# Splitting an MLP's matrix products into 64x64 pieces on the quarters of the TensorE array, in a kernel that runs a recurrence beside it

**Chip, cores, metric.** One core of one Trainium2 chip. The metric is device time in microseconds (us) of the whole kernel; lower is better. A profile of one execution is read beside the times.

## The reference

A linear recurrence for 4 x 8 heads, 768 steps, head width 40, and then an MLP over the 3072 tokens of 320 channels:

```python
for t in range(S):                       # S = 768, D = 40, 32 heads
    y[t]  = r[t] @ state
    Sa    = state @ a[t]
    state = state * w[t] - outer(Sa, b[t]) + outer(v[t], k[t])
x = y as (3072, 320)
h = x @ w_in                             # (320, 2048), float32
g = h * sigmoid(1.702 * h)
out = g @ w_out                          # (2048, 320)
```

## The kernel before

The recurrence is done in chunks of 128 steps: 6 chunks x 4 batches = 24 "units". Each unit has a main chain (`solve`: `first`, 14 `level` pieces, then `back`, `update`, `scores`, `read`, `bridge`). Spread between its pieces lie the preparation of the next unit (`prep`: four transposed operands, the triangular products called "scores" RV, A, NT and N, and the turned state; the chain's own `scores` are called M) and the MLP of an earlier pair of units: `up` beside even units, `down` beside odd ones. The order of all instructions is fixed by the program. The program deals out eight PSUM tiles of 128 x 512 float32, called banks here, as rings:

```python
ps_misc  = ctx.enter_context(tc.tile_pool(name="ps_misc",  bufs=3, space=PSUM))   # scores, transposes, update, read, bridge
ps_solve = ctx.enter_context(tc.tile_pool(name="ps_solve", bufs=3, space=PSUM))   # first, level
ps_mlp   = ctx.enter_context(tc.tile_pool(name="ps_mlp",   bufs=2, space=PSUM))
...
def score(dst, lhsT, rhs, low=False):          # takes two banks: the row halves write one each
    ps = [quad(psum(ps_misc)) for _ in range(2)]
    for q in range(NP):
        for e in range(2):
            p = slice(e * DP, (e + 1) * DP)    # partitions 0-63, 64-127
            mm(ps[e][:, q, :], lhsT[p, q, :], rhs[p, q, :], q == 0)
    nc.vector.tensor_tensor(dst[0], ps[0], lower4 if low else upper4, ALU.mult)
    nc.scalar.copy(dst[1], ps[1])
    ...
def up(j):                                     # 256 tokens; 16 steps
    def step(f):
        ph = psum(ps_mlp)[:, :2 * C]
        for kt, (o, n) in enumerate(KT):       # 320 = 128 + 128 + 64
            nc.tensor.matmul(ph, w_in_sb[:n, kt, f * 128:(f + 1) * 128], xTs[j][:n, kt, :],
                             start=kt == 0, stop=kt == NK - 1)
        sg = ...; nc.scalar.activation(sg, ph, ACT.Sigmoid, scale=1.702)
        g = ...;  nc.vector.tensor_mul(g, ph, sg)
    return [lambda f=f: step(f) for f in range(NF)]

def down(j):                                   # 2 units x 4 parts
    def step(u, part):
        if part == 0:
            po[u] = psum(ps_mlp)[:, :DM]
        for f in range(part * NF // 4, (part + 1) * NF // 4):
            nc.tensor.matmul(po[u], gTs[j][f][:, u * C:(u + 1) * C], w_out_sb[:, f, :],
                             start=f == 0, stop=f == NF - 1)
        ...
# per unit:
weave(solve(i), mixed(*[l for l in (side, mlp) if l]))   # side = prep of the next unit, and decays
```

The weights come as float64 bits and are rounded to float32 beside the first two units, in pieces, by VectorE and GpSimd.

Of the kernel before, what the change touches and what calls it, by code (L numbers as in the profile page):

```python
# [15 lines left out]
FP32 = mybir.dt.float32  # L16
# [5 lines left out]

# The recurrence, for one head and a chunk of C = 128 steps, with F_t the product of the decays
# from the middle of the chunk up to t (exclusive; its inverse before the middle), per key channel:
#
#   S_t = Z_t diag(F_t),  kh = k / F_{t+1},  bh = -b / F_{t+1},  ah = a F_t
#   A = tril(ah kh^T, -1),  N = tril(ah bh^T, -1)
#   SA = (I - N)^-1 (A v + ah Z_0^T)
#   Z_C = Z_0 + v^T kh + SA^T bh
#   y  = F (r Z_0 + tril(r v^T, -1) kh + tril(r SA^T, -1) bh)  # L30
#
# The decays are positive, so F is the exponential of a sum of logarithms, which a product with a
# constant triangle takes; the middle as its origin keeps F and 1 / F small over the chunk.
# N is nilpotent, so (I - N)^-1 = (I + N)(I + N^2)(I + N^4) ... (I + N^64) exactly.
# Two heads share the 128 partitions of a channel-major tile, 64 apiece, the rest zeros.


def weave(main, side):
    """Issue main in order, with side spread evenly through it."""
    done = 0  # L40
    for i, f in enumerate(main):
        f()
        upto = len(side) * (i + 1) // len(main)
        while done < upto:
            side[done]()
            done += 1
# [3 lines left out]
def rwkv7_gelu_quick(ctx: ExitStack, tc: tile.TileContext, rT_d, k_d, v_d, w_d, a_d, b_d, w_in, w_out, out):  # L50
    nc = tc.nc
    B, S, H, D = k_d.shape
    DM = H * D
# [6 lines left out]
    NF = DFF // 128  # L60
    KT = [(o, min(128, DM - o)) for o in range(0, DM, 128)]
    NK = len(KT)
    PIECE = max(256, DM)
    LEVELS = C.bit_length() - 1
    assert S % C == 0 and H % 2 == 0 and B % 2 == 0 and D <= DP and DFF % 128 == 0 and DM <= 512

    ctx.enter_context(tc.manual_schedule())
    const = ctx.enter_context(tc.tile_pool(name="const", bufs=1))
    work = ctx.enter_context(tc.tile_pool(name="work", bufs=2))
    ps_misc = ctx.enter_context(tc.tile_pool(name="ps_misc", bufs=3, space=bass.MemoryType.PSUM))  # L70
    ps_solve = ctx.enter_context(tc.tile_pool(name="ps_solve", bufs=3, space=bass.MemoryType.PSUM))
    ps_mlp = ctx.enter_context(tc.tile_pool(name="ps_mlp", bufs=2, space=bass.MemoryType.PSUM))

# [10 lines left out]
    def mm(o, lhsT, rhs, start):  # L84
        nc.tensor.matmul(o, lhsT, rhs, start=start, stop=True, skip_group_check=True)  # L85

# [1 line left out]
    ident = single("ident", [128, 128])  # L88
# [8 lines left out]
                            pattern=[[-1, 128]], channel_multiplier=1)  # L97
    # [u, t]: 1 where u <= t, less 1 where u is before the middle
    cums = single("cums", [128, 128])
# [12 lines left out]

# [1 line left out]
    nat = [single(f"nat{i}", [128, 4, H, DP]) for i in range(2)]  # L114
# [17 lines left out]

    w_in_sb = single("w_in_sb", [128, NK, DFF])
    w_out_sb = single("w_out_sb", [128, NF, DM])

# [1 line left out]
    def load_weight(dst, src):  # L137
        P, n = dst.shape
        raw = work.tile([128, PIECE], INT64, tag="raw", name="raw")
        nc.sync.dma_start(raw[:P, :n], src)  # L140
        word = lambda dt: raw[:P, :n].bitcast(dt).rearrange("p (n two) -> p n two", two=2)
        lo, hi = word(UINT32)[:, :, 0], word(INT32)[:, :, 1]
        scale = work.tile([128, PIECE], INT32, tag="scale", name="scale", bufs=1)[:P, :n]
        frac = work.tile([128, PIECE], INT32, tag="frac", name="frac", bufs=1)[:P, :n]
        # 2 ** exponent with the sign: 0 below the range of float32, infinite above
        nc.vector.tensor_scalar(scale, hi, 20, 0x7FF, ALU.logical_shift_right, ALU.bitwise_and)  # L146
        nc.gpsimd.tensor_scalar(scale, scale, 896.0, 0.0, ALU.subtract, ALU.max)  # L147
        nc.gpsimd.tensor_scalar(scale, scale, 255.0, 2.0 ** 23, ALU.min, ALU.mult)  # L148
        nc.vector.scalar_tensor_tensor(scale, in0=hi, scalar=-2 ** 31, in1=scale,  # L149
                                       op0=ALU.bitwise_and, op1=ALU.bitwise_or)  # L150
        # the significand, in units of 2 ** -20
        nc.vector.tensor_scalar(frac, hi, 0xFFFFF, 0x100000, ALU.bitwise_and, ALU.bitwise_or)  # L152
        nc.vector.scalar_tensor_tensor(dst, in0=lo, scalar=2.0 ** -32, in1=frac, op0=ALU.mult, op1=ALU.add)  # L153
        nc.vector.scalar_tensor_tensor(dst, in0=dst, scalar=2.0 ** -20, in1=scale.bitcast(FP32),
                                       op0=ALU.mult, op1=ALU.mult)

    def load_weights():
        pieces = [(w_in_sb[:n, kt, f:f + 256], w_in[o:o + n, f:f + 256])
                  for f in range(0, DFF, 256) for kt, (o, n) in enumerate(KT)]
        pieces += [(w_out_sb[:, f, :], w_out[f * 128:(f + 1) * 128, :]) for f in range(NF)]  # L160
        return [lambda d=d, s=s: load_weight(d, s) for d, s in pieces]

    units = [(c, b) for c in range(NCH) for b in range(B)]
    ins, ws, Fs, Gs, st = {}, {}, {}, {}, {}

# [1 line left out]
    def load(i):  # L167
# [15 lines left out]

# [1 line left out]
    def decay(i):  # L185
# [22 lines left out]

# [1 line left out]
    def score(dst, lhsT, rhs, low=False):  # L210
# [11 lines left out]
    def turn(dst, src, copy):  # L222
        """The four [128, 128] blocks of src, transposed."""
        ps = quad(psum(ps_misc))
        for q in range(NP):
            nc.tensor.transpose(ps[:, q, :], src(q), ident)  # L226
        copy(dst, ps)
# [42 lines left out]

# [1 line left out]
    def solve(i):  # L272
# [57 lines left out]
        def read():  # L330
# [7 lines left out]
            for h in range(H):  # L338
                mm(Y[:, h], s["M"][h % 2][:, h // 2], nt[:, 1, h, :D], False)
            s["x"] = work.tile([128, DM], FP32, tag="x", name="x")  # L340
            nc.vector.tensor_mul(s["x"], Y.rearrange("t h d -> t (h d)"), Fs.pop(i))

        def bridge():
            if i % 2 == 0:
                xTs[i // 2] = work.tile([128, NK, 2 * C], FP32, tag="xT", name="xT")
            xT, at = xTs[i // 2], slice(i % 2 * C, (i % 2 + 1) * C)
            ps = psum(ps_misc)[:, :NK * C].rearrange("p (k t) -> p k t", k=NK)
            for kt, (o, n) in enumerate(KT):
                nc.tensor.transpose(ps[:n, kt], s["x"][:, o:o + n], ident)
            full = sum(n == 128 for _, n in KT)  # L350
            nc.vector.tensor_copy(xT[:, :full, at], ps[:, :full])  # L351
            if full < NK:
                nc.scalar.copy(xT[:KT[full][1], full, at], ps[:KT[full][1], full])
            del st[i]
# [3 lines left out]

# [1 line left out]
    xTs, gTs = {}, {}  # L360

    def up(j):
        gTs[j] = []

        def step(f):
            ph = psum(ps_mlp)[:, :2 * C]
            for kt, (o, n) in enumerate(KT):
                nc.tensor.matmul(ph, w_in_sb[:n, kt, f * 128:(f + 1) * 128], xTs[j][:n, kt, :],  # L368
                                 start=kt == 0, stop=kt == NK - 1)
            sg = work.tile([128, 2 * C], FP32, tag="sg", name="sg")  # L370
            nc.scalar.activation(sg, ph, ACT.Sigmoid, scale=1.702)  # L371
            g = work.tile([128, 2 * C], FP32, tag="g", name="g", bufs=NF + 2)
            nc.vector.tensor_mul(g, ph, sg)  # L373
            gTs[j].append(g)
        return [lambda f=f: step(f) for f in range(NF)]

    def down(j):
        po = {}

        def step(u, part):  # L380
            if part == 0:
                po[u] = psum(ps_mlp)[:, :DM]
            for f in range(part * NF // 4, (part + 1) * NF // 4):
                nc.tensor.matmul(po[u], gTs[j][f][:, u * C:(u + 1) * C], w_out_sb[:, f, :],  # L384
                                 start=f == 0, stop=f == NF - 1)
            if part == 3:
                c, b = units[2 * j + u]
                ob = work.tile([128, DM], FP32, tag="ob", name="ob")
                nc.scalar.copy(ob, po.pop(u))
                nc.sync.dma_start(out[b * S + c * C:b * S + (c + 1) * C, :], ob)  # L390
        return [lambda u=u, part=part: step(u, part) for u in range(2) for part in range(4)]

    def mixed(*lists):
        """One list, each given list spread evenly over it."""
        return [f for _, _, f in sorted(((n + 0.5) / len(l), m, f) for m, l in enumerate(lists)
# [50 lines left out]
```

## Time and profile before

| | before |
|---|---|
| time, median of 2 runs | 2012.28 us (2008.07 to 2016.5) |
| profiled span | 1992.4 us, mean granted TensorE clock 0.935 |
| TensorE busy | 1863.5 us of it |
| MLP products | 1152 up and 768 down instructions of 13608 |
| half-rate clock after the second unit | 107 us |

Most of the profile's lines are shown with the prediction. The last row is a sum over the trace's own list of clock changes: every entry of it is 1.0 or 0.5, and I add up the stretches at half rate that begin after the second unit's bridge (245 us), where the recurrence and the MLP run in full. Of a stretch at half rate I count at most half its length as lost (sixteen products of 40 columns took 3.55 us in one, shown below, against 1.92 at full clock). The profiled execution is not one of the two that were timed and ran some 20 us faster than they did; in a later round an execution of the same kernel at 2013.92 us had a mean granted clock of 0.923, which makes some 50 us more at half rate. So 107 us is at the low end for this kernel.

The end of a unit in the kernel before, from its timeline (start us, length us, instructions; in brackets idle time just before, and what ended it):

```profile
1186.75 1.16 PE L85 MATMUL bank<-rT,sT 64*128 64x128 f32 x16
...
1188.69 1.16 PE L85 MATMUL bank<-bT,aT 64*128 64x128 f32 x14 [0.56 <-DVE M L216]
1189.77 1.98 PE L85 MATMUL bank<-nat,RV 128*128 128x40 f32 x16
1191.58 1.10 PE L85 MATMUL bank<-zT,rT 128*128 128x80 f32 x8
1192.51 1.92 PE L85 MATMUL bank<-nat,M 128*128 128x40 f32 x16
...
1197.99 0.63 PE L226 MATMUL bank<-ident,z 128*128 128x128 f32 x4 [1.01 <-DVE z L259]
1198.46 1.76 PE L85 MATMUL bank<-nat,A 128*128 128x40 f32 x15
```

There are two waits, one inside the N scores and one before the state's transposes. Between and after them come products with only 40 or 80 columns, which start 0.112 us apart as the products of 128 columns do in this trace (medians at full clock). Products of 320 columns start 0.269 us apart and those of 256 columns 0.216; from these I estimate 0.83 ns a column (0.053 us for 64), so 40 columns stream in some 0.03 us.

### The profile page before, as it was taken

How to read it: one execution, taken by the hardware profiler on the slowest of the kernel's cores; microseconds unless marked ns; L12 is line 12 of the kernel's file. 1: busy time of each engine (PE TensorE's matmuls, PEld its weight loads, DVE VectorE, ACT ScalarE, POOL GpSimd, SP SyncE). 2: the span in 40 equal slices, each digit the busy share in tenths (PEclk: the TensorE clock that was granted, in tenths of full speed). 3: DMA queues.
4: the chain of work that ended last, by engine and by line, in shares of the span. 5: the costliest groups of instructions: out<-in, count | busy, mean ns of one | idle time of the engine just before them, and what ended most of it. 6: DMA issues, size and time to landing. Idle time of an engine off the chain costs nothing.

```text
span 1992.4 us, 31126 instructions
## 1 busy us (share of the span) xinstructions
PE 1863.5 (94%) x13608; PEld 1604.9 (81%) x13608; DVE 630.5 (32%) x1380; ACT 435.0 (22%) x872; POOL 206.4 (10%) x266
## 2 busy tenths in 40 slices
PE   6756599999999999999999999999999999999999
PEld 5756587887988888888788888788788788898885
DVE  4444432232223323223323223323323332323221
ACT  2101022222112322112322112322222222212211
POOL 3454510000000000000000000000000000000000
PEclk9758688998999999889999899999999998999999
DMA  2121200010010010010001001001001001000000
GB/s 81 46 68 39 81 8 1 5 50 1 4 37 1 1 54 1 1 40 1 1 20 35 1 5 37 1 5 50 1 4 37 1 4 37 1 4 21 1 4 11
DMA packets 34281, 40.02 MB, mean 20 GB/s; under 512 B 3424, under 2 KB 29536, under 8 KB 34144
## 3 DMA queue, kind: packets, MB, share of 16 engines
q1 hardware_dynamic: 34144, 38.02, 6.2%
q8 instruction: 107, 1.75, 0.4%
q14 instruction: 30, 0.25, 0.0%
HBM read 34.08 MB, written 3.93 MB: 19 GB/s over the span
## 4 chain that ended last, share of the span: by engine, by line
PE 87%; DVE 6%; POOL 4%; issue 2%; ACT 1%; ACTq 0%; POOLq 0%; DVEq 0%
PE bank L85 57%; PE bank L368 15%; PE bank L384 11%; PE bank L226 3%; POOL scale L148 2%; POOL scale L147 2%; DVE scale L149 1%; DVE M L216 1%; DVE frac L152 1%; DVE w_in_sb L153 0%; DVE scale L146 0%; ACT logw L190 0%; DVE w_out_sb L153 0%; DVE N L309 0%; DVE xT L351 0%
## 5 line engine op out<-in xcount | busy, mean ns | idle before, releaser
L85 PEld LDWEIGHTS bank<-xs,NT 128*128 128x128 f32 x2688 | 343.2, 198 | 66.7 <-issue 41.8
L85 PE MATMUL bank<-xs,NT 128*128 128x40 f32 x2688 | 360.4, 285 | 17.6 <-DVE xs L286 10.3
L85 PE MATMUL bank<-NT,N 128*128 128x128 f32 x2304 | 342.7, 294 | 31.7 <-DVE xs L302 31.6
L368 PE MATMUL bank<-xT,w_in_sb 128*128 128x256 f32 (+1 forms) x1152 | 334.7, 414 | 0.0
L85 PEld LDWEIGHTS bank<-NT,N 128*128 128x128 f32 x2304 | 293.8, 200 | 33.2 <-DVE xs L302 32.9
L298 ACT COPY NT<-bank 128x512 f32<-128x512 f32 x288 | 168.8, 586 | 672.8 <-PE bank L85 672.8
L309 DVE COPY N<-bank 128x512 f32<-128x512 f32 x240 | 165.8, 691 | 341.0 <-PE bank L85 340.9
L368 PEld LDWEIGHTS bank<-xT,w_in_sb 128*128 128x128 f32 (+1 forms) x1152 | 194.1, 195 | 90.7 <-issue 77.6
L85 PE MATMUL bank<-N,NT 128*128 128x128 f32 x1920 | 266.3, 284 | 0.0
L85 PEld LDWEIGHTS bank<-N,NT 128*128 128x128 f32 x1920 | 246.7, 201 | 0.0
L384 PE MATMUL bank<-w_out_sb,g 128*128 128x320 f32 x768 | 227.8, 442 | 0.0
L384 PEld LDWEIGHTS bank<-w_out_sb,g 128*128 128x128 f32 x768 | 141.7, 194 | 48.9 <-issue 3.1
L373 DVE TENSOR_TENSOR g<-bank,sg 128x256 f32<-128x256 f32 x192 | 81.5, 425 | 300.6 <-ACT sg L371 300.6
L371 ACT ACTIVATE sg<-bank 128x256 f32<-128x256 f32 x192 | 73.7, 384 | 364.1 <-PE bank L368 364.1
L302 DVE TENSOR_TENSOR xs<-xs,bank 128x160 f32<-128x160 f32 x288 | 91.8, 319 | 161.0 <-PE bank L85 157.4
L219 POOL TENSOR_SCALAR_AFFINE_SELECT RV<-RV 128x512 f32<-128x512 f32 x24 | 15.6, 650 | 762.9 <-ACT RV L217 762.9
L226 PE MATMUL bank<-ident,nat 128*128 128x128 f32 x384 | 60.9, 284 | 0.2 <-DVE RV L216 0.2
L85 PE MATMUL bank<-nat,RV 128*128 128x40 f32 x384 | 50.9, 295 | 8.1 <-DVE M L216 8.1
L147 POOL TENSOR_SCALAR scale<-scale 128x256 int32<-128x256 int32 (+2 forms) x40 | 46.4, 1160 | 109.2 <-DVE scale L146 109.2
L85 PEld LDWEIGHTS bank<-nat,RV 128*128 128x128 f32 x384 | 48.1, 203 | 11.6 <-DVE M L216 8.7
L85 PE MATMUL bank<-nat,M 128*128 128x40 f32 x384 | 56.6, 315 | 0.0
L219 POOL TENSOR_SCALAR_AFFINE_SELECT A<-A 128x512 f32<-128x512 f32 x24 | 15.9, 663 | 382.2 <-DVE A L216 296.5
(102 smaller groups left out, 1453.6 us busy)
## 6 DMA issues: line engine op xcount, KB each, us to landing
raw<-in_w_out SPq DMA_DIRECT2D x16, 320.0 KB
raw<-in_w_in SPq DMA_DIRECT2D x16, 256.0 KB
in_w<-in_w SPq DMA_DIRECT2D x24, 160.0 KB
in_k<-in_k SPq DMA_DIRECT2D x24, 160.0 KB
in_b<-in_b SPq DMA_DIRECT2D x24, 160.0 KB
in_a<-in_a SPq DMA_DIRECT2D x24, 160.0 KB
in_v<-in_v SPq DMA_DIRECT2D x24, 160.0 KB
rT<-in_rT SPq DMA_DIRECT2D x48, 80.0 KB
```

What stands on the lines that cost most here:

```text
L85: nc.tensor.matmul(o, lhsT, rhs, start=start, stop=True, skip_group_check=True)
L147: nc.gpsimd.tensor_scalar(scale, scale, 896.0, 0.0, ALU.subtract, ALU.max)
L148: nc.gpsimd.tensor_scalar(scale, scale, 255.0, 2.0 ** 23, ALU.min, ALU.mult)
L219: nc.gpsimd.affine_select(out=dst[1], in_=dst[1], compare_op=ALU.is_gt, fill=0.0, base=0, pattern=[[0, NP], [s, 128]], channel_multiplier=-s)
L226: nc.tensor.transpose(ps[:, q, :], src(q), ident)
L298: nc.scalar.copy(s["NT"][e], ps)
L302: nc.vector.tensor_add(new, xs[e], dx)
L309: nc.vector.tensor_copy(s["N"][e], ps)
L368: nc.tensor.matmul(ph, w_in_sb[:n, kt, f * 128:(f + 1) * 128], xTs[j][:n, kt, :], start=kt == 0, stop=kt == NK - 1)
L371: nc.scalar.activation(sg, ph, ACT.Sigmoid, scale=1.702)
L373: nc.vector.tensor_mul(g, ph, sg)
L384: nc.tensor.matmul(po[u], gTs[j][f][:, u * C:(u + 1) * C], w_out_sb[:, f, :], start=f == 0, stop=f == NF - 1)
```

## The change

The contraction of 320 does not divide by 128, so a third of the up product's instructions (384 of 1152 in the trace) are half-height pieces, 64x128. With 64x64 pieces 320 = 5 x 64, and four pieces (two row halves, two column halves) run at a time. The program places activations and weights in both partition halves for that: `x` is written twice, the bridge makes five doubled blocks, and `w_in` is laid out so that the upper and the lower half belong to different blocks of hidden channels. The program lets the row halves write different banks, so each MLP step takes two; the MLP's ring grows to three at the cost of the miscellaneous ring.

```diff
-    ps_misc = ctx.enter_context(tc.tile_pool(name="ps_misc", bufs=3, space=bass.MemoryType.PSUM))
+    ps_misc = ctx.enter_context(tc.tile_pool(name="ps_misc", bufs=2, space=bass.MemoryType.PSUM))
-    ps_mlp = ctx.enter_context(tc.tile_pool(name="ps_mlp", bufs=2, space=bass.MemoryType.PSUM))
+    ps_mlp = ctx.enter_context(tc.tile_pool(name="ps_mlp", bufs=3, space=bass.MemoryType.PSUM))
... (w_in laid out as [128, 5, 8, 128]; 36 instead of 40 pieces of weights) ...
-            s["x"] = work.tile([128, DM], FP32, tag="x", name="x")
-            nc.vector.tensor_mul(s["x"], Y.rearrange("t h d -> t (h d)"), Fs.pop(i))
+            s["x"] = work.tile([128, NK, 2, 64], FP32, tag="x", name="x", bufs=1)
+            nc.vector.tensor_mul(s["x"], twice(Y.rearrange("t h d -> t (h d)")), twice(Fs.pop(i)))
... (bridge: 5 transposes into two banks instead of 3 into one) ...
-        def step(f):
-            ph = psum(ps_mlp)[:, :2 * C]
-            for kt, (o, n) in enumerate(KT):
-                nc.tensor.matmul(ph, w_in_sb[:n, kt, f * 128:(f + 1) * 128], xTs[j][:n, kt, :],
-                                 start=kt == 0, stop=kt == NK - 1)
+        def step(m):
+            ph = [psum(ps_mlp)[:, :2 * C] for _ in range(2)]
+            for k in range(NK):
+                for c in range(2):
+                    for r in range(2):
+                        nc.tensor.matmul(ph[r][halves_of[c]], w_in_sb[halves_of[r], k, m, c * 64:(c + 1) * 64],
+                                         xTs[j][halves_of[r], k, :], start=k == 0, stop=k == NK - 1)
... (sigmoid and product for both banks) ...
-        return [lambda f=f: step(f) for f in range(NF)]
+        return [lambda m=m: step(m) for m in range(NF // 2)]
...
-                po[u] = psum(ps_mlp)[:, :DM]
+                po[u] = [psum(ps_mlp)[:, :DM] for _ in range(2)]
-                nc.tensor.matmul(po[u], gTs[j][f][:, u * C:(u + 1) * C], w_out_sb[:, f, :],
-                                 start=f == 0, stop=f == NF - 1)
+                for c in range(2):
+                    for r in range(2):
+                        o = u * C + c * 64
+                        nc.tensor.matmul(po[u][r][halves_of[c]], gTs[j][f][halves_of[r], o:o + 64],
+                                         w_out_sb[halves_of[r], f, :], start=f == 0, stop=f == NF - 1)
-                nc.scalar.copy(ob, po.pop(u))
+                two = po.pop(u)
+                nc.scalar.copy(ob, two[0])
+                nc.vector.tensor_add(ob, ob, two[1])
```

More of the change, by code (lines that the diff above doesn't have):

```diff
@@ L60, in rwkv7_gelu_quick @@
     NF = DFF // 128
-    KT = [(o, min(128, DM - o)) for o in range(0, DM, 128)]
-    NK = len(KT)
+    NK = DM // 64
     PIECE = max(256, DM)
     LEVELS = C.bit_length() - 1
-    assert S % C == 0 and H % 2 == 0 and B % 2 == 0 and D <= DP and DFF % 128 == 0 and DM <= 512
+    assert S % C == 0 and H % 2 == 0 and B % 2 == 0 and D <= DP and DFF % 256 == 0 and DM <= 512 and DM % 64 == 0
     ctx.enter_context(tc.manual_schedule())
@@ L131, in rwkv7_gelu_quick, with load_weight @@
         nc.gpsimd.memset(t[:, :, :, D:], 0.0)
-    w_in_sb = single("w_in_sb", [128, NK, DFF])
+    w_in_sb = single("w_in_sb", [128, NK, NF // 2, 128])
     w_out_sb = single("w_out_sb", [128, NF, DM])
-    def load_weight(dst, src):
+    def load_weight(dst, *srcs):
         P, n = dst.shape
         raw = work.tile([128, PIECE], INT64, tag="raw", name="raw")
-        nc.sync.dma_start(raw[:P, :n], src)
+        for i, src in enumerate(srcs):
+            rows = slice(i * P // len(srcs), (i + 1) * P // len(srcs))
+            to = raw[rows, :n]
+            nc.sync.dma_start(to if len(src.shape) == 2 else
+                              to.rearrange("p (m f) -> p m f", m=src.shape[1]), src)
         word = lambda dt: raw[:P, :n].bitcast(dt).rearrange("p (n two) -> p n two", two=2)
@@ L157, in load_weights @@
     def load_weights():
-        pieces = [(w_in_sb[:n, kt, f:f + 256], w_in[o:o + n, f:f + 256])
-                  for f in range(0, DFF, 256) for kt, (o, n) in enumerate(KT)]
+        blocks = w_in.rearrange("(k p) (m r f) -> k r p m f", p=64, r=2, f=128)
+        pieces = [(w_in_sb[:, k, m:m + 2].rearrange("p m f -> p (m f)"),
+                   blocks[k, 0][:, m:m + 2], blocks[k, 1][:, m:m + 2])
+                  for m in range(0, NF // 2, 2) for k in range(NK)]
         pieces += [(w_out_sb[:, f, :], w_out[f * 128:(f + 1) * 128, :]) for f in range(NF)]
-        return [lambda d=d, s=s: load_weight(d, s) for d, s in pieces]
+        return [lambda p=p: load_weight(*p) for p in pieces]
     units = [(c, b) for c in range(NCH) for b in range(B)]
@@ L339, in read @@
                 mm(Y[:, h], s["M"][h % 2][:, h // 2], nt[:, 1, h, :D], False)
-            s["x"] = work.tile([128, DM], FP32, tag="x", name="x")
-            nc.vector.tensor_mul(s["x"], Y.rearrange("t h d -> t (h d)"), Fs.pop(i))
+            s["x"] = work.tile([128, NK, 2, 64], FP32, tag="x", name="x", bufs=1)
+            twice = lambda t: t.rearrange("t (k d) -> t k d", k=NK).unsqueeze(2).to_broadcast([128, NK, 2, 64])
+            nc.vector.tensor_mul(s["x"], twice(Y.rearrange("t h d -> t (h d)")), twice(Fs.pop(i)))
         def bridge():
@@ L346, in bridge @@
             xT, at = xTs[i // 2], slice(i % 2 * C, (i % 2 + 1) * C)
-            ps = psum(ps_misc)[:, :NK * C].rearrange("p (k t) -> p k t", k=NK)
-            for kt, (o, n) in enumerate(KT):
-                nc.tensor.transpose(ps[:n, kt], s["x"][:, o:o + n], ident)
-            full = sum(n == 128 for _, n in KT)
-            nc.vector.tensor_copy(xT[:, :full, at], ps[:, :full])
-            if full < NK:
-                nc.scalar.copy(xT[:KT[full][1], full, at], ps[:KT[full][1], full])
+            for k0 in range(0, NK, 4):
+                n = min(4, NK - k0)
+                ps = psum(ps_misc)[:, :n * C].rearrange("p (k t) -> p k t", k=n)
+                for k in range(n):
+                    nc.tensor.transpose(ps[:, k], s["x"][:, k0 + k].rearrange("t e d -> t (e d)"), ident)
+                (nc.vector.tensor_copy if n == 4 else nc.scalar.copy)(xT[:, k0:k0 + n, at], ps)
             del st[i]
@@ L360, in rwkv7_gelu_quick @@
     xTs, gTs = {}, {}
+    halves_of = [slice(0, 64), slice(64, 128)]
     def up(j):
         gTs[j] = []
-        def step(f):
-            ph = psum(ps_mlp)[:, :2 * C]
-            for kt, (o, n) in enumerate(KT):
-                nc.tensor.matmul(ph, w_in_sb[:n, kt, f * 128:(f + 1) * 128], xTs[j][:n, kt, :],
-                                 start=kt == 0, stop=kt == NK - 1)
-            sg = work.tile([128, 2 * C], FP32, tag="sg", name="sg")
-            nc.scalar.activation(sg, ph, ACT.Sigmoid, scale=1.702)
-            g = work.tile([128, 2 * C], FP32, tag="g", name="g", bufs=NF + 2)
-            nc.vector.tensor_mul(g, ph, sg)
-            gTs[j].append(g)
-        return [lambda f=f: step(f) for f in range(NF)]
+        def step(m):
[6 more added lines that the diff above has]
+            for r in range(2):
+                sg = work.tile([128, 2 * C], FP32, tag="sg", name="sg")
+                nc.scalar.activation(sg, ph[r], ACT.Sigmoid, scale=1.702)
+                g = work.tile([128, 2 * C], FP32, tag="g", name="g", bufs=NF + 2)
+                nc.vector.tensor_mul(g, ph[r], sg)
+                gTs[j].append(g)
+        return [lambda m=m: step(m) for m in range(NF // 2)]
     def down(j):
@@ L381, in step @@
             if part == 0:
-                po[u] = psum(ps_mlp)[:, :DM]
+                po[u] = [psum(ps_mlp)[:, :DM] for _ in range(2)]
             for f in range(part * NF // 4, (part + 1) * NF // 4):
-                nc.tensor.matmul(po[u], gTs[j][f][:, u * C:(u + 1) * C], w_out_sb[:, f, :],
-                                 start=f == 0, stop=f == NF - 1)
+                for c in range(2):
+                    for r in range(2):
+                        o = u * C + c * 64
+                        nc.tensor.matmul(po[u][r][halves_of[c]], gTs[j][f][halves_of[r], o:o + 64],
+                                         w_out_sb[halves_of[r], f, :], start=f == 0, stop=f == NF - 1)
             if part == 3:
```

## The prediction

Five passages that no trace or run of this case shows are cut from the text below, each cut marked. None held a term of the sum: all eight stand, -68 + 30 + 0 - 15 + 4 + 61 + 3 + 12 = +27 us, and 2012 + 27 = 2039 us. The two halves of a half-height score start 0.007 us apart, as do two 40-column halves of the decays' sums, the next two 0.06 us later. That a quarter piece streams as long as a full product, and that its changes of mode cost what those of the half-height pieces cost, was my estimate.

> **What bounds the kernel now.** I read the page first, then the TensorE groups with shapes apart, then the timeline at a few places. From the page, the busy shares, the slices and the chain that ended last:
>
> ```profile
> PE 1863.5 (94%) x13608; PEld 1604.9 (81%) x13608; DVE 630.5 (32%) x1380; ACT 435.0 (22%) x872; POOL 206.4 (10%) x266
> ...
> PE   6756599999999999999999999999999999999999
> ...
> PEclk9758688998999999889999899999999998999999
> ...
> PE 87%; DVE 6%; POOL 4%; issue 2%; ACT 1%; ACTq 0%; POOLq 0%; DVEq 0%
> ```
>
> TensorE is the bound, except in the first five slices (250 us). The MLP is a quarter of its work. Its groups (count, busy us, mean ns):
>
> ```profile
> L384 PE MATMUL bank<-w_out_sb,g 128*128 128x320 f32 x768 | 227.8, 442 | 0.0
> L368 PE MATMUL bank<-xT,w_in_sb 128*128 128x256 f32 x768 | 213.7, 402 | 0.0
> L368 PE MATMUL bank<-xT,w_in_sb 64*128 64x256 f32 x384 | 136.8, 437 | 0.0
> ```
>
> Each float32 product is two instructions (1152 = 2 x 3 x 16 x 12). Busy means overlap, so I take spacings. The timeline's end is the MLP alone (start, length, count):
>
> ```profile
> 1944.94 26.95 PE L368 MATMUL bank<-xT,w_in_sb 128*128 128x256 f32 x96
> 1971.83 17.49 PE L384 MATMUL bank<-w_out_sb,g 128*128 128x320 f32 x64
> ```
>
> Down: 17.4/64 = 0.27 us an instruction. Up: 26.95/16 = 1.685 us for a slice of 128 hidden channels (6 instructions). Within it, same-shape instructions start 0.216 us apart, so 6 x 0.216 = 1.30; the other 0.39 is two changes between the full array and the half-height piece (the third tile of 320 = 128+128+64). One change is 0.1 us before the next weight load plus 0.1 us of that load uncovered. So **0.2 us a change**.
>
> In the first 245 us the chain is the conversion of the weights, a relay between VectorE and GpSimd. One of 40 such pieces, from the chain in order of time:
>
> ```profile
> 92.08 1.09 POOL scale L147
> 93.24 1.09 POOL scale L148
> 94.36 0.42 DVE scale L149
> 95.02 0.44 DVE w_in_sb L153
> ```
>
> The w_in pieces take 4.2 us each, also those of 64 rows.
>
> Last, a wait that the change will multiply. The timeline near the end of a unit:
>
> ```profile
> 870.72 1.16 PE L85 MATMUL bank<-rT,sT 64*128 64x128 f32 x16
> ...
> 871.72 0.38 PE L85 MATMUL bank<-bT,aT 64*128 64x128 f32 x2
> 871.91 0.69 DVE L216 TENSOR_TENSOR M<-bank,upper 128x512 f32<-128x512 f32 x1 [2.79 <-PE bank L85]
> ...
> 872.66 1.16 PE L85 MATMUL bank<-bT,aT 64*128 64x128 f32 x14 [0.56 <-DVE M L216]
> ```
>
> Two score products follow each other; the second needs a bank that VectorE is still emptying, and TensorE stands from 871.83 to 872.66. This is the ring of three miscellaneous PSUM banks running out (two banks for a score, two for the next). The first block also shows that two halves of the array run together: 16 half-height instructions in about 1.0 us, 0.06 us each, against 0.11 for full ones of the same width.
>
> [...] No instruction here uses 64x64; the sums of the decays (40-column halves) run two abreast, but with two columns of data. [...] The trace has half-rate stretches beyond the start in slices 10, 17, 18, 23 and others, all near the ends of units.
>
> **The change part by part.**
> *Arithmetic.* A quarter piece does a quarter of a full product in the same streaming time, so four abreast only break even. The gain is padding: 320 = 5 x 64, so two hidden slices cost 5 x 2 quartets of instructions (10 x 0.216 = 2.16 us) where they cost 12 x 0.216 = 2.59. Down has no padding and gains nothing.
> *Changes of mode, up.* Before: 4 for two slices, 2 x 1.685 = 3.37 us. After: one into quarters and one out, 2.16 + 0.38 = 2.54. So -0.83 a step, 8 steps for 256 tokens: -6.6, less 0.4 where a score product used to share the half-height mode: -6.2. Eleven groups lie beside the recurrence: **-68 us**.
> *Changes of mode, down.* None before; now every one of 8 parts enters and leaves: +0.38 x 8, less 0.2 next to scores, x 11 = **+30 us**.
> *Last group.* Up: no changes, 8 x 2.16, but three banks at two a step let the next step wait for sigmoid and product of the one before (0.41 + 0.42 + 0.42 + 0.06 from the last matmul's start, less 0.22: 1.1 us), x 7: 25.0 against 26.95. Down waits twice for a bank (1.7) and its result takes one VectorE addition more (0.5). About **0**.
> *Weights.* 36 pieces instead of 40; the chain there is serial, so 4 x 4.2 = 17; I take **-15**.
> *Bridge.* 5 transposes instead of 3: 2 x 0.11 x 22 = **+4** (the doubled VectorE product is covered by the MLP step that follows the read).
> *Two miscellaneous banks instead of three.* This is the largest term. After the change up and down both have 8 steps, so every unit ends in the order that odd units show today: transposes of SA, NT scores, update, MLP, M scores, N scores, read, MLP, bridge, state. In a ring of two: NT's second bank waits for the copy of the SA transposes (0.59 us copy plus latencies: 0.75); the update waits for VectorE's emptying of NT (0.3 + 0.69 + 0.06, less the 0.2 of the change: 0.85); N waits as today; the read waits for N's emptying (0.85); state waits 0.25 more as the bridge's copy is longer. Sum 2.7 us. Of units 2 to 22, 13 have this order (35); 5 have the decays too and a shifted order, in which the product after the read and the bridge wait as well, 4.35 (22); the 3 of the last chunk have no update, 1.5 (4.5). **+61 us**. Bursts of two evictions in the up units: +3.
> *Clock.* The new waits lie in the same ends of units where the narrow 40-column matmuls already let the clock drop; half-rate time after the start is now some 110 us, so 50 us lost. A few more drops at some 6 us each: **+12**, a guess.
>
> Sum: -68 + 30 + 0 - 15 + 4 + 61 + 3 + 12 = +27 us. 2012 + 27 = **2039 us**.
>
> **The rivals.** (a) *The ring of two costs little*, because pieces between hide it. Against: the blocks stand back to back, as in the lines above[...]. If half of it is hidden and the clock is as before, the sum is about -15: 1997 us. If all: 1955. (b) *Quarters do not run four abreast*[...]. Then up and down stream twice as long, 12 x (17.3 + 17.2) = 410 us more: some 2430. For: nothing here has 64x64 with wide data. Against: the sums pair up[...]. I give it 6%. (c) *Issue becomes the bound*: 8 instructions in 0.216 us is 27 ns each. Against: half-height scores issue 4 in 0.111, the same rate, without a gap. (d) *More idle time drops the clock at nearly every unit end*: another 20 to 40 us, 2070.
>
> **Range and chances.** The terms of +61 and -38 (up and down) may each be off by a third, the clock by 20: about 35 us in all, with (b) as a tail. 80%: 1990 to 2090. The 2% limits are 1972 and 2052.5: faster 0.07, within 0.59, slower 0.34.
>
> **What would show it.** In the changed profile: quartets of quarter matmuls starting within 0.03 us, and 0.22 (up) and 0.27 us (down) from quartet to quartet; some 2.5 us for each up step and for each down part; the weight conversion over some 15 us sooner; new idle time of TensorE released by NT, N and sT evictions at unit ends, 2 to 4 us a unit; about as many or more half-rate slices. Wrong if unit ends show no such waits (then faster), if a step takes 4 us or more (b), or if a change into quarters costs far from 0.2 us: there are about 350 of them, so 0.1 us on each is 35 us.

## The result

The changed kernel takes 2152.65 us (2150.78 to 2154.52, 2 runs) against 2012.28: ratio 1.072, 95% interval 1.062 to 1.082. It is slower by 140 us, where 27 were predicted and 2090 was the upper end of the range. Ratios here and below are the mean time of one kernel's fast runs over that of the other's of the same rounds, so not quite the ratio of the medians quoted.

Rows of the page for the changed kernel (busy, clock by slices, chain):

```profile
PE 1966.1 (91%) x18648; PEld 1656.7 (77%) x18648; DVE 632.0 (29%) x1384; ACT 423.8 (20%) x872; POOL 197.1 (9%) x258
...
PEclk9657598897989979989979979989899997898899
...
PE 84%; DVE 8%; POOL 3%; ACT 2%; issue 2%; ACTq 0%; POOLq 0%; DVEq 0%
```

The clock's row is the one that changed most: of the last 34 slices 14 stand at 7 or 8, where 6 did (mean granted clock 0.877 against 0.935). Half-rate time after the second unit is 368 us against 107.

The pure MLP at the end, in the timeline of the changed kernel:

```profile
2104.02 2.39 PE L384 MATMUL bank<-xT,w_in_sb 64*64 64x256 f32 x40 [0.93 <-DVE g L390]
2107.34 2.39 PE L384 MATMUL bank<-xT,w_in_sb 64*64 64x256 f32 x40 [0.93 <-DVE g L390]
...
2127.25 8.84 PE L404 MATMUL bank<-w_out_sb,g 64*64 64x320 f32 x128 [0.82 <-DVE g L390]
```

Forty quarter instructions take as long as ten full ones: in the trace's records the four of a quartet start within 0.021 us of each other, and quartets 0.216 us apart. Full instructions of 256 columns start 0.216 us apart in the kernel before, so a quartet takes what one of them took: the quarters do run four abreast. The wait for the sigmoid and the product is there as predicted.

The end of a unit in the changed kernel, in the same order as the one shown before, with the NT scores and the update ahead of it:

```profile
1247.55 1.16 PE L84 MATMUL bank<-aT,bT 64*128 64x128 f32 x14 [0.26 <-ACT sT L234]
1249.28 1.12 PE L84 MATMUL bank<-nat 128*128 128x80 f32 x8 [0.58 <-DVE NT L223]
...
1253.54 1.16 PE L84 MATMUL bank<-rT,sT 64*128 64x128 f32 x16
1255.48 1.16 PE L84 MATMUL bank<-bT,aT 64*128 64x128 f32 x16 [0.78 <-DVE M L223]
1257.42 1.98 PE L84 MATMUL bank<-nat,RV 128*128 128x40 f32 x16 [0.78 <-DVE N L223]
1259.22 1.91 PE L84 MATMUL bank<-zT,rT 128*128 128x80 f32 x8
1260.92 3.55 PE L84 MATMUL bank<-nat,M 128*128 128x40 f32 x16
1264.41 4.55 PE L404 MATMUL bank<-w_out_sb,g 64*64 64x320 f32 x32
1268.88 1.06 PE L361 MATMUL bank<-ident,x 128*128 128x128 f32 x5
1271.11 0.63 PE L233 MATMUL bank<-ident,z 128*128 128x128 f32 x4 [1.16 <-DVE z L266]
```

The predicted new waits are there: in the NT scores (0.26 us, ended by the copy of the SA transposes), before the update (0.58, ended by the emptying of NT) and before the read (0.78, ended by the emptying of N). But look at the lengths: from 1259 us the same instructions take nearly twice as long. Sixteen `nat,M` products take 3.55 us instead of 1.92, and an MLP part 4.55 instead of 2.38. Stretches around this place, changed kernel and then kernel before (stretch, its length, busy us and count of PE, PEld, DVE, ACT, POOL, then the granted clock):

```profile
1200.00:1255.00 55.00, 53.87 (x569) 43.65 (x567) 14.60 (x29) 10.15 (x19) 1.90 (x3) 1.00 0.01 4
1255.00:1290.00 35.00, 32.16 (x219) 27.60 (x220) 7.42 (x16) 4.11 (x9) 2.54 (x4) 0.66 0.17 52
```

```profile
1180.00:1205.00 25.00, 23.43 (x186) 19.92 (x185) 5.18 (x11) 4.14 (x9) 3.19 (x5) 1.00 0.24 70
1205.00:1260.00 55.00, 55.00 (x410) 46.44 (x409) 19.59 (x41) 14.56 (x29) 1.27 (x2) 1.00 0.01 2
```

At this unit's end the clock fell twice (for 10.24 us from 1259.31 and for 13.65 us from 1272.96), to a mean of 0.66 over 35 us, with no wait over 1.2 us; in the kernel before it held at 1.00. From 250 us to the end, the stretch views give these sums:

```profile
250.00:2149.00 1899.00, 1789.35 (x17596) 1494.40 (x17594) 520.96 (x1106) 389.17 (x804) 97.25 (x151) 0.90 0.04 13
```

```profile
250.00:1992.00 1742.00, 1702.39 (x12538) 1455.45 (x12537) 513.40 (x1083) 400.79 (x805) 97.59 (x151) 0.96 0.05 14
```

TensorE's idle time rose from 40 to 110 us, that is by 70, of which about 8 lie in the last MLP group. That is near the predicted 61 us of waits. Its busy time rose by 87 us; if the MLP's steps became cheaper by the predicted 38, about 125 us more of its time is the same work at a slower clock. Half the additional half-rate time is (368 - 107)/2 = 130, which agrees. These two executions differ by 157 us, not by 140, since the profiled one of the kernel before was a fast one.

### The profile page after: what moved, and what is told of

The parts are those of the page before. It is cut to its first block, busy times and chain, and to the rows that moved or that the text cites. A ratio compares the mean times of both kernels' runs of the same rounds, so it can differ in the third digit from the quotient of the medians.

```text
span 2149.1 us, 41259 instructions
## 1 busy us (share of the span) xinstructions
PE 1966.1 (91%) x18648; PEld 1656.7 (77%) x18648; DVE 632.0 (29%) x1384; ACT 423.8 (20%) x872; POOL 197.1 (9%) x258
## 4 chain that ended last, share of the span: by engine, by line
PE 84%; DVE 8%; POOL 3%; ACT 2%; issue 2%; ACTq 0%; POOLq 0%; DVEq 0%
PE bank L84 58%; PE bank L384 11%; PE bank L404 11%; PE bank L233 3%; POOL scale L153 2%; POOL scale L152 2%; DVE g L390 1%; DVE NT L223 1%; DVE M L223 1%; ACT sg L388 1%; DVE N L223 1%; DVE scale L154 1%; DVE xT L362 1%; ACT sT L234 0%; PE bank L361 0%
## 5 line engine op out<-in xcount | busy, mean ns | idle before, releaser
L84 PE MATMUL bank<-xs,NT 128*128 128x40 f32 x2688 | 378.0, 293 | 18.1 <-DVE xs L293 12.9
L84 PE MATMUL bank<-NT,N 128*128 128x128 f32 x2304 | 359.1, 303 | 22.3 <-DVE xs L309 22.3
L84 PEld LDWEIGHTS bank<-NT,N 128*128 128x128 f32 x2304 | 309.0, 208 | 23.6 <-DVE xs L309 23.6
L384 PE MATMUL bank<-xT,w_in_sb 64*64 64x256 f32 x3840 | 250.4, 406 | 6.6 <-DVE g L390 6.5
L404 PE MATMUL bank<-w_out_sb,g 64*64 64x320 f32 x3072 | 249.5, 467 | 1.3 <-DVE g L390 0.8
L384 PEld LDWEIGHTS bank<-xT,w_in_sb 64*64 64x64 f32 x3840 | 146.4, 143 | 78.2 <-issue 16.0
L404 PEld LDWEIGHTS bank<-w_out_sb,g 64*64 64x64 f32 x3072 | 116.1, 143 | 92.9 <-issue 21.7
L84 PE MATMUL bank<-nat,M 128*128 128x40 f32 x384 | 81.8, 398 | 0.0
L84 PEld LDWEIGHTS bank<-nat,M 128*128 128x128 f32 x384 | 80.8, 319 | 0.0
L350 DVE TENSOR_TENSOR x<-bank,F 128x640 f32<-128x640 f32 x24 | 19.8, 824 | 158.6 <-PE bank L84 158.6
```

The source lines that it names most:

```text
L84: nc.tensor.matmul(o, lhsT, rhs, start=start, stop=True, skip_group_check=True)
L384: nc.tensor.matmul(ph[r][halves_of[c]], w_in_sb[halves_of[r], k, m, c * 64:(c + 1) * 64], xTs[j][halves_of[r], k, :], start=k == 0, stop=k ...
L404: nc.tensor.matmul(po[u][r][halves_of[c]], gTs[j][f][halves_of[r], o:o + 64], w_out_sb[halves_of[r], f, :], start=f == 0, stop=f == NF - 1)
```

## The experiments

The question was no longer whether the steps were right but why the clock fell so much more often. The theories: **W**, the waits that come with the ring of two banks; **Q**, the quarter pieces themselves count little to what grants the clock; later **C**, the eight coarse up steps leave the ends of units without wide products. Every version gave correct results. The half-rate column counts the stretches that begin after the second unit's bridge, in one profiled execution of each version; executions of one version differ. "Before" is the median of the kernel before in the same rounds, slow runs included; the ratios leave slow runs out.

| version | time, us (median) | before | ratio (95%) | half rate, us |
|---|---|---|---|---|
| kernel before | - | - | 1 | 107 |
| changed kernel | 2153 | 2012 | 1.072 (1.062-1.082) | 368 |
| before, two misc banks | 2164 | 2014 | 1.078 (1.071-1.086) | 348 |
| changed, three misc banks | 2022 | 2014 | 1.007 (0.999-1.016) | 255 |
| up alone in quarters, three banks | 1968 | 2014 | 0.982 (0.976-0.989) | 187 |
| changed, waits filled | 2040 | 2014 | 1.016 (1.009-1.024) | 114 |
| before, up steps in 8 pairs | 2069 | 2003 | 1.034 (1.026-1.041) | 263 |
| changed, three banks, up steps split | 1978 | 2003 | 0.989 (0.981-0.998) | 122 |
| changed, three banks, filled | 1970 | 2003 | 0.985 (0.979-0.992) | 112 |
| up alone, three banks, filled | 1936 | 2003 | 0.965 (0.956-0.974) | 106 |
| before, filled | 1986 | 1996 | 0.996 (0.990-1.001) | 61 |
| up alone, three banks, state first | 1981 | 1996 | 0.991 (0.984-0.997) | 178 |
| the same, filled | 2000 | 1996 | 1.002 (0.998-1.006) | 195 |
| up alone, three banks, state second | 1919 | 1995 | 0.951 (0.945-0.958) | 65 |

**1. The changed kernel with three miscellaneous banks.**

```diff
-    ps_misc = ... bufs=2 ...
+    ps_misc = ... bufs=3 ...
-    ps_mlp = ... bufs=3 ...
+    ps_mlp = ... bufs=2 ...
```

> The changed kernel, with the banks of PSUM given back: three miscellaneous banks, two for the MLP. Two theories of the 140 us lost. W: the ring of two makes TensorE wait at the ends of units, and the windows with waits let its clock drop (half-rate time after the first two units 107 us before the change, 368 us after it). Q: quarter pieces themselves count little to whatever grants the clock. W expects half-rate time of 80 to 170 us and about 1950 to 1985 us in all (before, less 38 for the MLP's steps, a little for the first units, more for the last MLP group). Q expects half-rate time above 250 us and 2060 to 2110 us, as only the waits themselves (60 us) go.

Measured: 2022 us, half-rate time 255 us. The half-rate time is as Q said, the time as neither did: most of the loss goes with the bank (131 us), but the clock did not come back to where it was, and the time lies 37 us above the upper end of W. The second unit's bridge began at 229.9 us, against 245.1 before the change and 244.2 with it; so the shorter conversion of weights is worth the predicted 15 us, and the ring of two had cost as much there.

**2. The kernel before with two miscellaneous banks.** Nothing in quarters; only the ring is cut.

```diff
-    ps_misc = ... bufs=3 ...
+    ps_misc = ... bufs=2 ...
-    ps_mlp = ... bufs=2 ...
+    ps_mlp = ... bufs=3 ...
```

> The kernel before, with only the ring of miscellaneous banks cut from three to two (the third goes to the MLP, which does not need it). W expects what the change showed: half-rate time over 250 us, 2140 to 2190 us. Q expects only the waits themselves: half-rate time about 110 us, 2060 to 2085 us.

Measured: 2164 us, half-rate time 348 us, as W said; Q's 2060 to 2085 falls. Its clock row:

```profile
PEclk9657598997998999899999789799799899898899
```

The bank alone, without any quarter piece, costs 7.8% (157 us between the means of the fast runs), as much as the whole change within the noise. In its trace the second bridge comes 14 us later than in the kernel before, and from 5 us after that bridge TensorE's idle time is 74 us against 40, so only some 35 more. Its busy time rose by 122 us with the same instructions, and half the additional half-rate time is (348 - 107)/2 = 120: most of the loss is the clock.

**3. Up in quarters, down as before, three banks.**

```diff
-                po[u] = [psum(ps_mlp)[:, :DM] for _ in range(2)]
+                po[u] = psum(ps_mlp)[:, :DM]
... (down's four quarter products and the addition back to one product and one copy)
```

> Only the up product in quarters, the down product as before the change, three miscellaneous banks. Both theories agree that the down product gains nothing from quarters and pays two changes of the array's mode a part, 30 us in all. W expects 1920 to 1960 us, some 25 to 30 us under the run with both products in quarters and three banks; Q expects half-rate time between those of that run and of the kernel before.

Measured: 1968 us, half-rate time 187 us. The down product in quarters costs 54 us (1968 against 2022). By the mean clocks of all four runs of each (0.902 to 0.912 and 0.913 to 0.917) some 20 of them are clock, and some 34 are left for the changes of mode, sized at 30. This version is faster than both kernels, if only by 1.8% (its interval lies under 1, but is not clear of the 2% that count as faster); the time lies just above what W said, and half-rate time again stayed above the kernel before's.

**4. The changed kernel with its waits filled.** All waits and both rings as changed; useless products of 512 columns, which write banks that nobody reads, stand where TensorE would be idle.

```diff
+    def fill(rows=False):
+        for e in range(2 if rows else 1):
+            p = slice(e * 64, e * 64 + 64) if rows else slice(0, 128)
+            mm(quad(psum(ps_solve)), upper[p], upper4[p], True)
...
+            fill()          # ahead of update, of read, of the state's transposes, of the NT scores
+            fill(True)      # ahead of the N scores
```

> The changed kernel with its two miscellaneous banks and all its waits, but with useless full-width products of 512 columns (0.85 us each) put ahead of the NT scores, the update, the N scores, the read and the state's transposes, where TensorE otherwise stands; nothing reads what they write. W, with the clock following how much of the array's time is used, expects half-rate time below 150 us and 2030 to 2080 us: more work and less time. If the waits themselves and not the clock cost the 140 us, or if Q holds and the clock stays low because of the quarter pieces, it expects 2150 us or more.

Measured: 2040 us, half-rate time 114 us. This is the cleanest separation: the kernel has the same rings and the same work, with useless products in five more places of most units, and is 113 us faster than without them. Its clock row, and the place that was shown at half rate before:

```profile
PEclk9767599989999999999989999999999899998999
```

```profile
1195.96 1.13 PE L84 MATMUL bank<-upper 128*128 128x512 f32 x2
1196.92 1.87 PE L84 MATMUL bank<-nat,RV 128*128 128x40 f32 x16
...
1207.57 1.02 PE L84 MATMUL bank<-upper 128*128 128x512 f32 x2
1208.90 0.63 PE L238 MATMUL bank<-ident,z 128*128 128x128 f32 x4 [0.30 <-DVE z L271]
```

The useless product stands in the place of the wait of 0.78 us before the read, and most of the one before the state's transposes. That it lands on the prediction's 2039 us is in part luck: the clock is about as before, but the 15 us of the weights were not gained, and the useless products are not as long as the waits that they fill (the next product starts 0.94 to 0.96 us after them at this unit's end; the 0.85 us of the expectation was an estimate, two instructions of 512 columns at 0.83 ns a column; the waits at the unit's end shown before were 0.26 to 1.16 us).

**5. The kernel before with its up steps in pairs.** After run 1, theory C: beside even units the kernel before has 16 up steps of 1.7 us, the changed one 8 of 2.5 us, so fewer of them fall among the narrow products.

```diff
-        return [lambda f=f: step(f) for f in range(NF)]
+        return [lambda f=f: (step(f), step(f + 1)) for f in range(0, NF, 2)]
```

> The kernel before, with its 16 up steps issued in 8 pairs, so that they lie among the recurrence as sparsely as the changed kernel's steps; nothing else changed, full array, three miscellaneous banks. The run with quarters and three banks had half-rate time of 255 us after the first two units against 107 us of the kernel before, and gained nothing. Theory C: 8 coarse steps leave the narrow products at the ends of the even units without wide ones between. C expects half-rate time of 180 to 260 us here and 2035 to 2075 us. Theory Q, that quarter pieces themselves count less to the clock, expects no change: about 107 us, 2000 to 2020 us.

Measured: 2069 us, half-rate time 263 us. C holds, at the edge of its range. Nothing but the order of the same instructions changed, on the full array with three banks, and it costs 3.4%. TensorE's idle time from 250 us on rose only from 40 to 47 us, so this is not a matter of waits:

```profile
PEclk9757597998999998889999789799999799998999
```

**6. Quarters, three banks, up steps in two parts.**

```diff
-            for k in range(NK):
+            for k in (range(3) if part == 0 else range(3, NK)):
...
-            for r in range(2):
+            for r in range(2 if part else 0):
-        return [lambda m=m: step(m) for m in range(NF // 2)]
+        return [lambda m=m, part=part: step(m, part) for m in range(NF // 2) for part in range(2)]
```

> Quarters for both products and three miscellaneous banks, with each up step issued in two parts (three of the five contraction pieces, then two), so that 16 parts spread as before the change. It pays 8 more pairs of changes of mode for 256 tokens, some 33 us. C expects half-rate time down from 255 to 110 to 180 us and about 1990 to 2015 us; Q expects half-rate time of about 250 us and 2040 to 2060 us.

Measured: 1978 us, half-rate time 122 us, a little better than C said. It pays for 8 more pairs of mode changes a group and is still faster than run 1 (ratio 0.989 against 1.007). So most of the 255 us of run 1 came from the coarse steps and not from the quarters: Q has no support left.

**7 and 8. Filling the two remaining waits** (N scores, state) with three banks, with both products in quarters and with up alone.

```diff
+            fill()          # ahead of the state's transposes
+            fill(True)      # ahead of the N scores
```

> Quarters for both products, three miscellaneous banks, and useless full-width products ahead of the N scores and of the state's transposes, the two places where TensorE still waits at each unit's end. If use of the array sets the clock, whatever the pieces: half-rate time below 130 us and 1950 to 1985 us, 40 to 70 us under the same kernel without them. If quarters themselves hold the clock down: above 200 us and no gain.

> The same useless products in the version with only the up product in quarters and three miscellaneous banks (1968 us, half-rate time 187 us without them). Expected: half-rate time below 100 us and 1915 to 1950 us, which would be the fastest so far.

Measured: 1970 us with 112 us at half rate, and 1936 us with 106 us. Both are as said in time; the second's half-rate time is a little above what was said. Filling took the first from a ratio of 1.007 to 0.985, the second from 0.982 to 0.965.

**9. The kernel before, filled in the same two places.**

> The kernel before, nothing in quarters, with the same useless products ahead of the N scores and of the state's transposes. It tells how much of the 1936 us of the version with up in quarters and such products is owed to the products alone. If use of the array sets the clock, half-rate time falls from 107 us to 30 to 80 us and the time by 0 to 25 us (1980 to 2005), as the products themselves cost some changes of mode; so most of the 1936 us would be the quarters' and not the filling's.

Measured: 1986 us against 1996, ratio 0.996, half-rate time 61 us. Where the clock was nearly full already, the useless products only pay for themselves. So run 8's gain over the kernel before, 3.5%, is not that of the useless products alone.

**10 and 11. Turning the next unit's state at the start of a unit,** so that the wait after the bridge goes without useless work; then the same with useless products ahead of the NT and N scores.

```diff
-        return [scale,
+        return [lambda: (scale(), state() if c > 0 else None),
...
-                ] + ([state] if c > 0 else [])
+                ]
```

> Up in quarters, three miscellaneous banks, no useless products; the next unit's state is turned at the start of the unit and not after the bridge, so that TensorE has no wait of 1.0 to 1.7 us there. Expected from the waits alone: 20 units by about 1.3 us, 26 us off 1968; with the clock (half-rate time from 187 to about 110 us) up to 40 more: 1910 to 1945 us.

> The version before this one with useless half-height products ahead of the NT and N scores, one of which lies after the bridge now. Half-rate time below 90 us; the products cost 2 by 22 by up to 0.9 us where they fill no wait, so 1900 to 1940 us.

Both missed: 1981 and 2000 us. The wait had only moved, and grown. The state's transposes now waited for their own product, which stood behind the scaling's two and the emptying of a level's product in VectorE's queue:

```profile
1105.45 0.66 PE L233 MATMUL bank<-ident,z 128*128 128x128 f32 x4 [1.99 <-DVE z L266]
```

A wait of 1.99 us in place of 1.1 to 1.7, now shortly after the narrow products of `first` and of the first level; half-rate time stayed at 178 and 195 us. I also had not counted that filling with the useless products elsewhere does nothing for this wait.

**12. The state's product at the start of the unit, its transposes one piece later.** Up in quarters, down on the full array, three miscellaneous banks, nothing useless.

```diff
-        def state():
+        def zmul():
             z = z0[i % 2]
             nc.vector.tensor_tensor(z[:, :, :, :D], zraw[b], ...)
+        def state():
+            z = z0[i % 2]
             s["zT"] = ...; turn(s["zT"], ..., nc.scalar.copy)
-        return [scale, turned("vT", ...), ..., ] + ([state] if c > 0 else [])
+        return [lambda: (scale(), zmul() if c > 0 else None)] + ([state] if c > 0 else []) + [turned("vT", ...), ...]
```

> The attempt to turn the state early failed because its transposes stood right behind their own product and two others on VectorE (a wait of 2.0 us in place of the one removed). Here the product is issued at the start of the unit and the transposes one piece later, so no wait should be left at that place; the N scores now lie after the bridge with a wait of some 0.5 us. Nothing useless is computed. Expected 1910 to 1950 us and half-rate time of 80 to 150 us against 1968 us and 187 us; if the wait at the bridge was not what drops the clock, it stays at 1960 us or more.

Measured: 1919 us (1890 to 1929; two of the four runs, at 1929, count as slow against the fastest), ratio 0.951 from the two fast ones; even the slow ones lie under every run of the kernel before in these rounds (1989 to 2003). With all four runs the ratio of the means is 0.959. The profiled execution, with 65 us at half rate, is the fastest of the four: its mean clock is 0.947, that of the others 0.935, 0.926 and 0.922, so the other three had some 50 to 100 us more at half rate. The end of a unit has one of its waits left, and no wait before `first`:

```profile
1105.84 1.16 PE L84 MATMUL bank<-aT,bT 64*128 64x128 f32 x14 [0.56 <-DVE M L223]
1106.93 1.98 PE L84 MATMUL bank<-nat,RV 128*128 128x40 f32 x16
...
1114.29 1.58 PE L84 MATMUL bank<-bT,aT 64*128 64x128 f32 x16
1115.80 1.98 PE L84 MATMUL bank<-nat,A 128*128 128x40 f32 x16
```

```profile
PEclk9858589999999999999999999999998999999999
```

It has the lowest median of all versions, 4.9% under the kernel before by its fast runs; its interval and that of run 8 (0.956 to 0.974) overlap. It has the padding saved by quarters in the up product, without the ring of two and the down product's changes of mode.

## Why the prediction was wrong

Its steps, one by one:

- **Four abreast, some 2.5 us for each up step and down part.** Right: 2.32 and 2.31 us from start to start, with 0.1 us more in the piece before and 0.1 in the piece after: the first quarter starts 0.205 us after a full product of 128 columns, where the next full one starts 0.112 after it, and the first full product 0.306 us after the last quartet of 256 columns, where the next quartet starts 0.216 after it. Into and out of the half-height pieces of 256 columns it was 0.309 for 0.216 and 0.306 for 0.216 in the kernel before. The net of up and down, -38 us, was not measured by itself. Runs 7 and 9, with the same useless products and three banks, allow an estimate: quarters are 20 us faster there (ratios 0.985 and 0.996), of which the weights give 15, while half-rate time of 112 against 61 us costs up to 25. That leaves -30, where -38 for the steps, 4 for the bridge and 4 for the last group make -30.
- **Last group, about 0.** From the last bridge to the end it is 53.6 against 50.0 us, so +4.
- **Weights, -15.** Right by itself (245.1 to 229.9 us with three banks), but given back whole in the changed kernel (244.2), since I counted the ring's waits for units 2 to 22 only; in run 2 the ring of two alone delays the second bridge by 14 us. A miss of 15 us.
- **Waits of the ring, +61.** Right in size: idle time rose by 62 us outside the last group. By place too, from start to start at full clock: from the NT scores to the update 2.48 us instead of 1.09, from the M scores to the read 3.88 instead of 3.03, and 0.4 more at the state beyond two more transposes, so 2.64 us for a unit's end where 2.7 were predicted. (The profile's idle time is another measure: it leaves out the end of the instruction before. It shows 0.56 us where the prediction reads 0.83.)
- **Clock, +12.** This is the step that failed. It said "A few more drops at some 6 us each". The changed kernel's half-rate time after the second unit rose by 261 us, worth up to 130 us of time, and filling the waits, with the quarters and the rings untouched, gave 113 us back. Of the 140 us between the medians, the other terms as measured or estimated here (-38, +4, 0 for the weights, +4 for the bridge, +62) leave 108. So the term is about 110 us, and up to 130 for the two profiled executions.

One slip of the sum, without effect on it: rival (a)'s "If all: 1955" should be 1963 (27 less 61, 3 and 12).

Rival (d), "More idle time drops the clock at nearly every unit end", named what happened, at 20 to 40 us more. What it named was right and the size was not, for two reasons. First, the number of drops: I had taken two or three more, and 37 stretches at half rate began after the second unit against 12 (without the one at the kernel's very end), mostly two around each end of a unit. The cost of one was about right: most lasted 7 to 14 us, so some 5 us lost. Second, the waits were not the only cause. The coarse steps alone, on the full array and with three banks, cost 66 us (run 5); I had noted that up would have 8 steps instead of 16 and used it for the order of the unit's end, but drew nothing from it for the clock.

The clock moves the time of one and the same kernel too: in the rounds of runs 5 to 8 two fast runs of the kernel before took 1983 us at a mean clock of 0.939 and 2010 us at 0.925, and 0.014 of 2000 us is the whole difference.

What goes with the drops is how much of the array's time is used, and a wait is only one way to lower it. To see this in the traces, I cut each into windows of 3.41 us (in the traces of the kernel before and of the changed kernel all changes of the clock lie at one phase of that period, and the half-rate stretches after the second unit, but for the one at the very end, last one to six periods, 3.41 to 20.48 us) and added up, for each window, the streaming time of its products (the estimate of 0.83 ns a column given above; a transpose counted half, a choice of mine that no trace shows), weighted by the share of the array that a piece covers, so a quarter counts a quarter. Taking the windows after 260 us that ran at full clock, in ten of the traces: of 375 windows with a use below 0.40, 219 were followed at once by a drop; of 4210 others, one. (In the four traces left out, those of runs 9 to 12, it is 83 of 124, and 4 of 1727. With transposes counted in full, the ten traces give 219 of 322, and 1 of 4263. The limit of 0.40 was chosen to fit these traces; it is not shown to be one of the chip's.) In the kernel before 30 of 474 windows were that low, in the changed one 62 of 442. The ends of units are near 0.40 without any wait: sixteen products of 40 columns start 0.11 us apart and stream for some 0.03 by the estimate. A wait of 0.8 us (0.23 of a window), or a missing wide step, can take one more window below it. That low use is a cause, and not only goes along with the drops, is shown as far as runs 4 and 7 show it: useless wide products in the waits took the half-rate time from 368 to 114 us and from 255 to 112. Why about two fifths of the low windows were not followed by a drop stays open.

Two points stay argued only. How the 131 us between the changed kernel and run 1 divide between the waits and the clock is worked out from idle and half-rate time, not run by itself: of 117 us between the two profiled executions, 14 lie before the second bridge, 39 are idle time and 63 busy time after it, and half the difference in half-rate time is (368 - 255)/2 = 56. And run 12 takes away a wait and moves the N scores behind the bridge at once; its gain over run 3 (0.951 against 0.982) is not divided between these.

I had counted the clock as a small correction to the sum (+12) and should have sized it as a rival to its largest terms.

## What to carry to other kernels

Where TensorE's work has narrow stretches, ask of every change what it does to the use of the array there, window by window (in these traces 219 of 375 windows of 3.41 us with a use below 0.40 were followed by a drop of the clock): here a bank taken from a ring cost about twice as much through the clock (some 110 us) as through the waits that it added (62 us), and wide steps made fewer and larger cost 3.4% with hardly any waits (7 us more). Take a tiling where it removes padding (the up product) and leave it where it only adds changes of mode (the down product, 54 us dearer in quarters with three banks). Before giving a PSUM bank away, walk the ring in program order and see which pieces stand back to back.
